# Loading and turning the first batch's keys in two halves of rows, with both sketch matrices on ScalarE's queue

## The chip, the cores and the metric

The kernel runs on one core of a Trainium2 chip. A core has TensorE (PE, matrix products; its weight loads are shown apart as PEld), VectorE (DVE), ScalarE (ACT), GpSimd (POOL) and SyncE (SP, which here only issues DMA transfers). Each engine works through its own instructions in order. ScalarE can issue transfers too. The metric is the device time of the whole program in microseconds, lower is better. A profile is one execution as the hardware profiler saw it; its times are microseconds from the first instruction.

## The reference

An attention with polynomial sketches, and then a SwiGLU block on its output:

```python
def phi(x):                                     # r = 8
    a = np.einsum('rd,bhsd->bhsr', S1, x)
    b = np.einsum('rd,bhsd->bhsr', S2, x)
    return np.einsum('bhsi,bhsj->bhsij', a, b).reshape(*x.shape[:-1], r * r)
q_p, k_p = (phi(q), phi(k))
kv = np.einsum('bhsf,bhsd->bhfd', k_p, v)
z = np.sum(k_p, axis=2)
num = np.einsum('bhsf,bhfd->bhsd', q_p, kv)
den = np.einsum('bhsf,bhf->bhs', q_p, z)[..., None] + 1e-06
attn = num / den
...
g = x @ w_gate                                  # x: attn as (B*S, H*D)
silu = g * (1.0 / (1.0 + np.exp(-g)))
val = x @ w_val
return (silu * val @ w_out)
```

There are 4 batches, 4 heads, 1088 positions and a head dimension of 32; x is 4352 x 128, and the hidden width is 1536. The keys, queries and values are float32. S1, S2 and the three weight matrices come as 64-bit floats; the kernel loads them as raw 64-bit words.

## The kernel before

**Stages.** The attention of batch 0 comes first and as fast as it can, since nothing else can be multiplied before it yields rows of x. Its queries go in three steps of 6, 5 and 6 groups of 64 positions. From the first step on, units of the SwiGLU block (two products, an activation, a product on VectorE) fill TensorE, at first with weights in float32 (L1025), later in split form (L989 to L1002, L1077). The attentions of batches 1 to 3 are woven into that stream. The program is scheduled by hand: the order in which the code calls the engines is their order of work.

**Transfers.** SyncE issues nearly all loads. Its first ones are, in this order: S1 (L201), all keys of batch 0 (`load_k(0)`, L164 and L207), the first third of the queries (L170 and L208), four pieces of the values (L176 and L209), then the first pieces of `wg` and `wv` (L199, called from L1188), the second third of the queries, the second pieces of `wg` and `wv`, and the last third of the queries (L185 to L189). ScalarE issues S2 (L202). The tile `sraw` takes S1 in its rows 0 to 7 and S2 in its rows 8 to 15.

**Layout of the keys.** `kld` has 128 partitions (4 heads by 32) and 36 slots of 32 elements, of which 34 are loaded and the last two are set to zero by GpSimd. The slot number is 9a + c, with a row a of 0 to 3 and a column c of 0 to 8 (NC = 9). The columns are worked on in three thirds, `fpieces`: c0 is columns 0 to 2, c1 is 3 to 5, and `aside` is 6 to 8.

**Sketches.** While the loads run, TensorE is kept busy with small products of a constant (`keep_warm`, L241; 98 of 32 columns and 12 of 64). `narrow` turns the raw words of both sketch matrices into float32: VectorE L263 and L264, ScalarE L268 and L269, VectorE L271, L277, L286. TensorE then copies the result to every head's partitions (L1165), followed by another `keep_warm` block (L1173 to L1175: 2 products of 512 columns, 7 of 32, 6 of 64). VectorE builds `s12`, a block diagonal form, from it (L1177), and ScalarE builds `sq` (L1183, L1184).

**Keys.** `turn_k` (L325) transposes blocks of 32 x 32 of the keys on VectorE, a third of the columns with all four rows at a time, in the order aside, c0, c1. `key_products` (L350) multiplies, for each column, the rows 0 and 1 together and the rows 2 and 3 together (`a` in 0, 2) with `s12`; each such product is two instructions in the profile. `key_copy` brings the result of a third out of PSUM on ScalarE (L368 for aside, L371 for the others). `key_features` forms the outer products: on GpSimd for aside, on VectorE for c0 and c1 (L377). VectorE turns the first queries (L333) between the key turns and these. TensorE multiplies the queries (L445) and then sums the features in the order c0, aside, c1 (L401); ScalarE copies the sums (L1217). `key_values` (L388) multiplies features and values, `totals` (L497) forms numerators and denominators, and `divide` ends with the first rows of x (L539). Between these VectorE also narrows the first weight pieces.

```python
    c0, c1, aside = fpieces
    order = [c for p in (c0, aside, c1) for c in range(*p)]
    for c in (aside, c0, c1):
        turn_k(*c)
    prods = {}
    for t, c in zip(("acc", "g1", "g2"), (aside, c0, c1)):
        ps = bank(t)
        key_products(ps, *c)
        prods[c] = key_copy(ps, *c, aside=(c == aside))
```

Of the kernel before, what the change touches and what calls it, by code (L numbers as in the profile page):

```python
# [19 lines left out]
def kernel(  # L20
# [28 lines left out]
    nc = tc.nc  # L49
    P = nc.NUM_PARTITIONS  # L50
    B, H, S, Dh = q.shape
    R = S1.shape[0]
    D, Dff = moe_w_gate.shape
    NT = B * S
    NX = S // 32
    HX = NX // 2
    NC = (NX + 3) // 4
# [39 lines left out]
    def touch(*which):  # L97
        for i in which:
            clock[0] += 1
            used[i] = clock[0]  # L100
# [11 lines left out]
    def bank(tag=None):  # L112

        if tag is not None:
            i = place[tag]
        else:
            i = place[free_banks[turn[0] % len(free_banks)]]
            turn[0] += 1
        touch(i)
        return PS[:, i, :]  # L120
# [17 lines left out]
    def wide(tag):  # L138
        i = place[tag]
        touch(i, i + 1)  # L140
        return PS[:, i : i + 2, :]
# [7 lines left out]
    sraw = const.tile([2 * R, Dh], S1.dtype, name="sraw")  # L149
# [3 lines left out]
    kld = const.tile([P, 4 * NC, Dh], FP32, tag="kld", name="kld", bufs=1)  # L153
    qld = const.tile([P, 4 * NC, Dh], FP32, tag="qld", name="qld", bufs=1)
    vld = const.tile([P, H, NC, Dh], FP32, tag="vld", name="vld", bufs=1)
    kT = const.tile([P, NC, 4, 32], FP32, tag="kT", name="kT", bufs=1)
# [3 lines left out]
    fpieces = ((0, 3), (3, 6), (6, NC))  # L160
    NRAW = 4

    def load_k(b):
        nc.sync.dma_start(  # L164
            out=kld[:, 0:NX, :], in_=k[b].rearrange("h (pp x) d -> (h pp) x d", pp=32)
        )

    def load_q(b, x0=0, x1=NX):
        src = q[b].rearrange("h (pp x) d -> (h pp) x d", pp=32)
        nc.sync.dma_start(out=qld[:, x0:x1, :], in_=src[:, x0:x1, :])  # L170
# [14 lines left out]
    def load_next():  # L185
# [12 lines left out]
        t = raw[name, i] = stage.tile([P, 3, P], I64, tag="raw", name="raw", bufs=NRAW)  # L198
        nc.sync.dma_start(out=t[:, 0 : c1 - c0, :], in_=part)  # L199

    nc.sync.dma_start(out=sraw[0:R, :], in_=S1)  # L201
    nc.scalar.dma_start(out=sraw[R : 2 * R, :], in_=S2)  # L202

    nc.gpsimd.memset(kld[:, NX : 4 * NC, :], 0.0)
    nc.gpsimd.memset(qld[:, NX : 4 * NC, :], 0.0)
    nc.gpsimd.memset(vld[96:128, :, NC - 2 : NC, :], 0.0)
    load_k(0)  # L207
    load_q(0, 0, 2 * XS)  # L208
    load_v(0, [nc.sync] * 4)  # L209

# [11 lines left out]
        out=ident[:], in_=ident[:], pattern=[[-1, P]], base=0, channel_multiplier=1,  # L222
# [12 lines left out]
    def keep_warm(n, w=TB, ps=None):  # L235


        if ps is None:
            ps = bank(free_banks[turn[0] % len(free_banks)])
        for _ in range(n):  # L240
            nc.tensor.matmul(  # L241
                ps[0:32, 0:w], warm[:, 0:32], warm[:, 0:w], start=True, stop=True
            )
# [78 lines left out]
    s123 = const.tile([P, 2 * H, 3, R], FP32, name="s123")  # L322
    own2 = const.tile([P, 2 * H], FP32, name="own2")
    sq = const.tile([P, 2, R, R], FP32, name="sq")
    def turn_k(c0, c1):  # L325
        four = "p (a c) d -> p a c d"
        nc.vector.transpose(
            out=kT[:, c0:c1, :, :].rearrange("p c a t -> p a c t"),
            in_=kld[:].rearrange(four, a=4)[:, :, c0:c1, :],
        )  # L330

    def turn_q(x0, n):
# [14 lines left out]
                    stop=True,  # L347
                )

    def key_products(ps, c0, c1):  # L350

        for c in range(c0, c1):
            for a in (0, 2):
                nc.tensor.matmul(  # L354
                    ps[32 * a : 32 * a + 64, 64 * (c - c0) : 64 * (c - c0) + 64],
                    kT[:, c, a : a + 2, :].rearrange("p a t -> p (a t)"),
                    s12[:].rearrange("p h t r -> p (h t r)"),
                    start=True,
                    stop=True,
                )  # L360

    def key_copy(ps, c0, c1, aside=False):

        n = c1 - c0
        ab = ps[:, 0 : 64 * n].rearrange("p (x t r) -> p x t r", t=2, r=R)
        if aside:
            kab = apool.tile([P, n * H, 2, R], FP32, tag="kab", name="kab")
            nc.scalar.copy(kab[:], ab)  # L368
            return kab[:, :, 0, :], kab[:, :, 1, :]
        ka = apool.tile([P, n * H, R], FP32, tag="ka%d" % c0, name="ka")  # L370
        nc.scalar.copy(ka[:], ab[:, :, 0, :])  # L371
        return ka[:], ab[:, :, 1, :]
# [194 lines left out]
    def turn_keys(b):  # L567

        for c in kpieces:
            turn_k(*c)  # L570
            if c[1] == NC and b + 1 < B:
                load_k(b + 1)
            yield
# [41 lines left out]
    def attentions():  # L615
# [5 lines left out]
        for i, c in enumerate(kpieces):  # L621
            key_products(kp[:, i, :], *c)
# [24 lines left out]
        kvz = pair("values")  # L647
        key_values(kvz[:, 0, 0:F], phk, 0, NC)
        kab, copies = sketched(pair(), key_products, 2, "kab2")
        run_copies(copies, 2)  # L650
        value_sums(kvz[:, 0, :], zs)
# [18 lines left out]
        for b in (2, 3):  # L670
            yield "pe"
            if b == 3:
                numerators(2, spread)
            kv = bank("g2")
            key_values(kv[:, 0:F], phk, 0, NC)
            if b == 2:
                kab, copies = sketched(pair(), key_products, 2, "kab2")
                run_copies(copies, 2)
            value_sums(kv, zs)
            fold(kv)  # L680
            spread = spread_out(b, kv)
            yield
            yield "pe"
            qab, copies = sketched(pair(), query_sketches, 3, "qab")
            run_copies(copies, 2)
            yield
            if b == 2:
                yield from turn_queries(3)
                phk = late[:, NL - 6 :, :].rearrange("p s (n h i j) -> p (s n) h i j", h=1, i=R, j=R)
                phk = phk.rearrange("p (c h) o i j -> p c (h o) i j", h=H)  # L690
                yield from features(phk, kab)
                zs, sums = feature_sums(phk)
            yield from beside(query_step(b, qab), sums)
# [105 lines left out]
    acc = {}  # L799
# [325 lines left out]
    rows = out.rearrange("(b pp x) (a d) -> b a pp x d", pp=32, x=NX, d=32)  # L1125
# [38 lines left out]
    for h in range(H):  # L1164
# [5 lines left out]
            stop=True,  # L1170
        )
    ps = bank("acc")
    keep_warm(2, ps=ps)  # L1173
    keep_warm(7, 32, ps=ps)
    keep_warm(6, 64, ps=ps)  # L1175
    sTv = srep[:, 0 : 2 * R].rearrange("p (t r) -> p t r", t=2)
# [1 line left out]
        out=s12[:],  # L1178
# [11 lines left out]

    c0, c1, aside = fpieces
    order = [c for p in (c0, aside, c1) for c in range(*p)]
    for c in (aside, c0, c1):
        turn_k(*c)
    prods = {}
    for t, c in zip(("acc", "g1", "g2"), (aside, c0, c1)):
        ps = bank(t)
        key_products(ps, *c)
        prods[c] = key_copy(ps, *c, aside=(c == aside))
    turn_q(*steps[0])  # L1200
    n = steps[0][1]
# [24 lines left out]
    ps = bank("g0")  # L1226
# [8 lines left out]
    ps = bank("g1")  # L1235
# [92 lines left out]
    for z, (i, j) in enumerate(seq):  # L1328
        if z == 17:
            free_banks.pop()  # L1330
            turn[0] %= 4
        unit(i, j)
        for p in parts.get(z, ()):
            part(*p)
        if z == 6:
            load_k(1)
            load_v(1, [nc.sync] * 4)
            load_q(1)
        if z >= 17:
            next_down()  # L1340
            parts_of(1)
        if z == 19:
            catch_up(nc.vector)
            catch_up(nc.vector)
        at(*steps_at.get(z, ()))
# [78 lines left out]
    ps = wide("a")[:, 0, 0:D]  # L1424
# [7 lines left out]
    b, x0 = divmod(t0 // 32, NX)  # L1432
# [34 lines left out]
```

## Time and profile before

| what | value |
| --- | --- |
| median of 3 runs | 276.63 us (276.59 to 276.78) |
| span of the profiled execution | 275.1 us |
| PE busy | 268.8 us, 98% of the span |
| DVE busy | 214.1 us, 78% |
| ACT busy | 193.6 us, 70% |
| POOL busy | 105.7 us, 38% |
| PE in the chain that ended last | 93% |
| mean granted TensorE clock | 0.999 |
| moved by DMA | 14.30 MB, mean 52 GB/s |

The time of a run is taken around the program, the span from its first to its last instruction, so the span is somewhat shorter. The profile's chain is found backwards from the last instruction: at each step to what released it, or to the instruction before it on its engine. A busy share is a mean over the span; what one stage waits for is read from the chain and the timeline of that stage. In a timeline line the first number is the start, the second the time from the first start to the last end of the merged instructions, and in brackets stands how long the engine was idle before, and what ended that.

### The profile page before, as it was taken

What the parts mean: (1) busy time and instruction counts of PE and PEld (TensorE: products, weight loads), DVE (VectorE), ACT (ScalarE), POOL (GpSimd) and SP (SyncE); (2) the same over time, 40 slices, a digit from 0 to 9 for tenths busy, and PEclk for the clock granted to TensorE, in tenths of its full rate; (3) what the DMA queues carried; (4) which work ended last, traced back from release to release, by engine and by line L of the source; (5) the groups of instructions that cost most, each with busy time, mean ns of one, the idle gap of its engine ahead of it and who ended that gap; (6) DMA issues with size and microseconds to landing.
All of it is one profiled execution on the core that took longest, in us unless ns stands there. A gap on an engine that the chain in (4) does not pass through costs nothing.

```text
span 275.1 us, 5788 instructions
## 1 busy us (share of the span) xinstructions
PE 268.8 (98%) x2191; PEld 200.5 (73%) x2191; DVE 214.1 (78%) x373; ACT 193.6 (70%) x349; POOL 105.7 (38%) x117
## 2 busy tenths in 40 slices
PE   7999999999999999999999999999999999999995
PEld 6645566666785786777577777867887888789994
DVE  3997988989788773887545766967987995998871
ACT  2468666462685686677479898769879888897880
POOL 3313422149350640260034353435535663553330
PEclk9999999999999999999999999999999999999999
DMA  6573196122231043000200020000100200010021
GB/s 191 172 216 87 49 270 200 60 104 62 62 88 23 4 111 99 2 0 0 38 12 4 1 38 0 0 2 11 26 2 0 36 1 0 13 25 1 2 36 29
DMA packets 26139, 14.30 MB, mean 52 GB/s; under 512 B 19840, under 2 KB 24192, under 8 KB 26112
## 3 DMA queue, kind: packets, MB, share of 16 engines
q1 hardware_dynamic: 25456, 13.84, 19.6%
q8 instruction: 17, 0.28, 0.4%
q10 hardware_dynamic: 656, 0.10, 0.2%
q14 instruction: 10, 0.08, 0.1%
HBM read 11.41 MB, written 2.23 MB: 50 GB/s over the span
## 4 chain that ended last, share of the span: by engine, by line
PE 93%; DVE 3%; DMA 2%; ACT 1%; issue 0%; SPq 0%
PE PS L1077 20%; PE PS L1001 14%; PE PS L989 14%; PE PS L1002 14%; PE PS L1025 12%; PE PS L1072 3%; PE PS L1071 3%; PE PS L1069 3%; PE PS L354 2%; PE PS L776 2%; PE PS L342 2%; DMA kld<-in_k_dram 2%; PE PS L388 2%; PE PS L1117 1%; PE PS L497 1%; PE PS L445 1%
## 5 line engine op out<-in xcount | busy, mean ns | idle before, releaser
L992 ACT ACTIVATE PS<-PS 128x960 f32<-128x960 f32 (+1 forms) x90 | 83.3, 926 | 29.8 <-PE PS L989 28.8
L1009 DVE SCALAR_TENSOR_TENSOR hbuf<-PS,sg 128x480 f32<-128x480 f32 (+1 forms) x87 | 55.2, 634 | 36.6 <-ACT sg L1004 36.1
L1004 ACT ACTIVATE sg<-PS 128x480 f32<-128x480 f32 (+1 forms) x90 | 49.6, 551 | 1.6 <-PE PS L1002 1.2
L1077 PE MATMUL PS<-hbuf,wo 128*128 128x480 f32 (+2 forms) x94 | 39.4, 516 | 0.0
L989 PE MATMUL PS<-xd,graw 128*128 128x480 f32 (+1 forms) x69 | 37.5, 543 | 0.0
L989 PE MATMUL PS<-xd,wd 128*128 128x480 f32 (+1 forms) x90 | 33.6, 373 | 0.0
L1002 PE MATMUL PS<-x,wb 128*128 128x480 f32 (+1 forms) x90 | 33.5, 372 | 0.0
L1001 PE MATMUL PS<-x,w 128*128 128x480 f32 (+1 forms) x90 | 33.4, 371 | 0.0
L1002 PE MATMUL PS<-x,graw 128*128 128x480 f32 (+1 forms) x69 | 25.5, 370 | 0.0
L989 PEld LDWEIGHTS PS<-xd,wd 128*128 128x128 f32 x90 | 17.0, 189 | 9.9 <-issue 5.3
L1025 PE MATMUL PS<-xT,wg 128*128 128x384 f32 (+1 forms) x60 | 23.5, 473 | 0.1
L1025 PE MATMUL PS<-xT,wv 128*128 128x384 f32 (+1 forms) x60 | 23.2, 467 | 0.3 <-DVE wv L286 0.3
L868 POOL TENSOR_TENSOR x<-xT,x 128x480 fp32r<-128x480 f32 (+1 forms) x6 | 7.2, 1195 | 37.8 <-ACT x L865 37.8
L1077 PEld LDWEIGHTS PS<-hbuf,wo 128*128 128x128 f32 x94 | 17.7, 189 | 5.4 <-issue 0.4
L1029 ACT ACTIVATE sg<-PS 128x384 f32<-128x384 f32 (+1 forms) x24 | 11.2, 468 | 13.2 <-PE PS L1025 12.4
L969 POOL TENSOR_TENSOR hlate<-hbuf,hlate 128x480 fp32r<-128x480 f32 (+1 forms) x12 | 14.6, 1218 | 11.0 <-ACT hlate L968 9.7
L989 PEld LDWEIGHTS PS<-xd,graw 128*128 128x128 f32 x69 | 13.0, 188 | 7.6 <-ACT PS L992 4.1
L1001 PEld LDWEIGHTS PS<-x,w 128*128 128x128 f32 x90 | 16.9, 187 | 2.2
L1002 PEld LDWEIGHTS PS<-x,wb 128*128 128x128 f32 x90 | 16.9, 188 | 2.1
L1001 PE MATMUL PS<-x,graw 128*128 128x480 f32 (+1 forms) x48 | 18.1, 376 | 0.0
L1077 PE MATMUL PS<-hbuf,scaled 128*128 128x480 f32 (+1 forms) x40 | 17.1, 518 | 0.0
L1025 PEld LDWEIGHTS PS<-xT,wv 128*128 128x128 f32 x60 | 11.2, 190 | 7.4 <-DVE hbuf L1040 0.8
(205 smaller groups left out, 572.0 us busy)
## 6 DMA issues: line engine op xcount, KB each, us to landing
kld<-in_k_dram SPq DMA_DIRECT2D x4, 544.0 KB, 4.4
vld<-in_v_dram SPq DMA_DIRECT2D x12, 144.0 KB, 4.3
qld<-in_q_dram SPq DMA_DIRECT2D x3, 544.0 KB, 4.8
raw<-in_moe_w_out_dram SPq DMA_DIRECT2D x4, 384.0 KB, 4.4
raw<-in_moe_w_gate_dram SPq DMA_DIRECT2D x3, 384.0 KB, 3.3
raw<-in_moe_w_val_dram SPq DMA_DIRECT2D x3, 384.0 KB, 3.5
out_dram<-o SPq DMA_DIRECT2D x16, 60.0 KB, 2.0
vld<-in_v_dram SPq DMA_DIRECT2D x4, 112.0 KB, 4.1
```

The lines of the kernel that those rows point to most:

```text
L969: add_to(before, y + 2, lambda: nc.gpsimd.tensor_tensor(out=h0, in0=h, in1=whole(h1), op=ALU.subtract))
L989: nc.tensor.matmul(ps[:, k], w_parts[id(w), j // 3][2][:, j % 3, :], xd, start=True, stop=True)
L992: nc.scalar.activation(ps, ps, AF.Copy, scale=-1.0 / WHOLE)
L1001: nc.tensor.matmul(ps[:, k], w1, x1, start=False, stop=False, skip_group_check=True)
L1002: nc.tensor.matmul(ps[:, k], wb, x0, start=False, stop=True, skip_group_check=True)
L1004: nc.scalar.activation(sg, ps[:, 0], AF.Silu, scale=WHOLE)
L1009: nc.vector.scalar_tensor_tensor(out=hj[:, 0:n], in0=ps[:, 1], scalar=WHOLE, in1=sg, op0=ALU.mult, op1=ALU.mult)
L1025: nc.tensor.matmul(o[:, 0:n], w[:, j, :], xT[:, t0 : t0 + n], start=True, stop=True)
L1029: nc.scalar.activation(sg[:, 0:n], g[:, 0:n], AF.Silu)
L1069: nc.tensor.matmul(acc[i][:, 0:n], wd, hd, **sides)
L1071: nc.tensor.matmul(p, w1, h1, start=(j == mine[0]), stop=False)
L1077: nc.tensor.matmul(acc[i][:, 0:n], w, hidden[i, j][:, 0:n], **sides)
```

## The change

Four things are changed, all in the work on batch 0 before its first features:

- `load_k` takes a range of slots. The keys of batch 0 are loaded by two transfers, slots 0 to 17 (rows a = 0, 1) and slots 18 to 33 (rows a = 2, 3), and these are the first two that SyncE issues. The other batches' keys are loaded whole, as before.
- S1 is issued by ScalarE, after S2.
- The keys are turned by four instructions instead of three: the rows 0 and 1 of all nine columns at once, then the rows 2 and 3 of aside, c0 and c1. TensorE multiplies the rows 0 and 1 of all three thirds first, and then the rows 2 and 3 of each third, after which that third is copied out.
- The second `keep_warm` block has one product of 512 columns instead of two.

```diff
-    def load_k(b):
-        nc.sync.dma_start(
-            out=kld[:, 0:NX, :], in_=k[b].rearrange("h (pp x) d -> (h pp) x d", pp=32)
-        )
+    def load_k(b, x0=0, x1=NX):
+        src = k[b].rearrange("h (pp x) d -> (h pp) x d", pp=32)
+        nc.sync.dma_start(out=kld[:, x0:x1, :], in_=src[:, x0:x1, :])
...
-    nc.sync.dma_start(out=sraw[0:R, :], in_=S1)
+    load_k(0, 0, 2 * NC)
+    load_k(0, 2 * NC, NX)
     nc.scalar.dma_start(out=sraw[R : 2 * R, :], in_=S2)
+    nc.scalar.dma_start(out=sraw[0:R, :], in_=S1)
...
-    load_k(0)
     load_q(0, 0, 2 * XS)
     load_v(0, [nc.sync] * 4)
...
-    def turn_k(c0, c1):
+    def turn_k(c0, c1, rows=slice(0, 4)):
         four = "p (a c) d -> p a c d"
         nc.vector.transpose(
-            out=kT[:, c0:c1, :, :].rearrange("p c a t -> p a c t"),
-            in_=kld[:].rearrange(four, a=4)[:, :, c0:c1, :],
+            out=kT[:, c0:c1, rows, :].rearrange("p c a t -> p a c t"),
+            in_=kld[:].rearrange(four, a=4)[:, rows, c0:c1, :],
         )
...
-    def key_products(ps, c0, c1):
+    def key_products(ps, c0, c1, rows=(0, 2)):
 
         for c in range(c0, c1):
-            for a in (0, 2):
+            for a in rows:
...
     ps = bank("acc")
-    keep_warm(2, ps=ps)
+    keep_warm(1, ps=ps)
     keep_warm(7, 32, ps=ps)
     keep_warm(6, 64, ps=ps)
...
-    for c in (aside, c0, c1):
-        turn_k(*c)
+    sums = dict(zip((aside, c0, c1), [bank(t) for t in ("acc", "g1", "g2")]))
+    turn_k(0, NC, slice(0, 2))
+    for c in sums:
+        turn_k(*c, slice(2, 4))
+    for c, ps in sums.items():
+        key_products(ps, *c, (0,))
     prods = {}
-    for t, c in zip(("acc", "g1", "g2"), (aside, c0, c1)):
-        ps = bank(t)
-        key_products(ps, *c)
+    for c, ps in sums.items():
+        key_products(ps, *c, (2,))
         prods[c] = key_copy(ps, *c, aside=(c == aside))
```

## The prediction

> **What bounds the kernel now.** I read the page first: PE is busy 98% of a 275.1 us span and 93% of the chain that ended last is PE, so a change in the opening is worth what it moves the point from which TensorE no longer waits. Then the chain of waits from 0 to 40 us, in order of time (start, duration, what):
>
> ```profile
> 1.24 4.45 DMA kld<-in_k_dram
> 5.69 0.02 issue
> 5.71 0.59 DVE kT L327
> 6.30 0.04 issue
> 6.34 1.49 PE PS L354 x36
> 7.83 0.92 PE PS L445 x32
> 8.76 0.04 issue
> 8.79 1.49 PE PS L401 x16
> 10.28 0.02 issue
> 10.30 0.38 ACT zq L1217
> ...
> 29.78 10.27 PE PS L1025 x33
> ```
>
> The opening hangs on the keys: 4.45 us from issue to landing, then turn, products, feature sums. From 14.62 to 22.20 this chain is VectorE without a gap, then TensorE to the end. So a shift at 5.71 is carried to the end almost one for one, unless something else arrives last. The timeline of the first 10 us shows what could (start, duration, engine, line):
>
> ```profile
> 0.84 0.57 ACTq L202 DMA_DIRECT2D sraw<-in_S_dram  x1
> ...
> 2.64 0.17 DVE L263 TENSOR_SCALAR exp<-sraw 16x32 int32<-16x32 int32 x1 [2.64 <-DMA sraw<-in_S_dram]
> ...
> 4.20 0.30 PE L1165 MATMUL PS<-ident,s 16*32 16x16 f32 x8
> 4.43 1.20 PE L241 MATMUL PS<-const-bfloat16-1.0 128*32 128x512 bf16 x15
> 4.64 0.23 DVE L1177 TENSOR_TENSOR s<-PS,own 128x64 f32<-128x64 f32 x1 [0.86 <-PE PS L1165]
> ...
> 5.71 1.50 DVE L327 STREAM_TRANSPOSE kT<-kld 128x384 f32<-128x384 f32 x3 [0.85 <-DMA kld<-in_k_dram]
> ```
>
> The sketches' way (landing, L263 to L286, TensorE L1165, VectorE L1177) ends at 4.87 and the keys come 0.85 us later. VectorE works in order and L1177 stands before the turns, in the changed kernel too: no half of the keys can be turned before the sketch matrices have made this whole way. That is the step on which everything turns.
>
> **The keys.** S1's issue (0.82 to 1.18) leaves SyncE's queue, so the keys are issued at 0.82, not 1.24: 0.42 us sooner. Two issues instead of one put the queries' issue back at 1.65, where it was. The first half is 18/34 of 544 KB, 288 KB. From 4 to 6 us the DMA window moves 0.60 MB, 300 GB/s; the other 256 KB cost 0.87 us there. First half: 0.82 + 4.45 - 0.87 = 4.40. Second half: between 0.82 + 4.45 = 5.27 (splitting costs nothing) and 1.24 + 4.45 = 5.69 (its own issue decides); I take 5.40, nearer the first, as the transfers queue behind one another.
>
> **The sketches.** S1 now goes second on ScalarE's queue: S2's issue lasts 0.57, so S1's starts near 0.84 + 0.57 + 0.05 = 1.46 (1.30 if the issue lasts 0.42, as each of ScalarE's two at 271.03 does, 0.88 together). From S2's issue to L263 it is 1.80 us (0.84 to 2.64): 3.26 for the new S1. But the keys are now in the 16 DMA engines before S1's packets; in the trace of before, the sketches' packets went ahead of them. No row shows a small transfer against a bulk one. Bounds: nothing (3.10 with the short issue), or behind the whole first half (4.40 + 0.10 = 4.50). I take one key packet in front, 0.17 us (a steady packet of 4,352 B lasts 0.168 us in the packet records), near the low bound because the two queues are separate: 3.43.
>
> The Trainium skill (DMA: Bandwidth & Descriptors, "Issuing engines are not separate DMA queues") says that DMAs from ScalarE and SyncE end on the same engines and interleave, and its section on queues has an engine finish a whole packet of one queue before it takes another's, some 9 to 17 descriptors. This speaks against the change: by it S1 would stand behind about a first half per engine, and the sum would go to the 4.50 above.
>
> From L263 on: 2.64 to 3.78 is 1.14; 0.06 to TensorE (as from a turn's end 6.29 to its product 6.34); L1165 to L1177 0.44 (4.20 to 4.64); 0.20 to the next VectorE instruction (L1177 lasts 0.23 and overlaps a little). 3.43 + 1.14 + 0.06 + 0.44 + 0.20 = 5.27 is T, the start of the first turn, against 5.71. Both key halves are covered: the first lands 0.87 before T, and the second's turns start at T + 0.70 = 5.97, 0.57 after its landing. With that cover gone the second half's delay would count in full. Were the halves not told apart and the first turn waited for all keys, T would be 5.42.
>
> **Turns and products.** Before, three turns of 384 elements start 0.47 apart ((7.13 - 5.71)/3); six products of a third start 0.058 apart after a first gap of 0.10; first product 0.16 after the turn's slot. TensorE is fed by the turns there, not the limit. After: a turn of 576 takes 0.70, three of 192 take 0.24 by proportion, or 0.30 if each has a fixed part; the four end 0 to 0.2 later than three, covered by what follows. Products of the first rows start at T + 0.70 + 0.16 = T + 0.86; nine of them end their starts at T + 1.37, and only then come those of the second rows: aside to T + 1.54, c0 to T + 1.72. The copy of a finished third starts 0.27 after its last product (6.69 to 6.96): aside T + 1.81, where before it was 1.25 after the first turn. GpSimd's features start 0.47 later (6.96 to 7.43) and last 1.51: T + 3.79. ScalarE's next copy comes at T + 2.03 and lasts 0.24; VectorE's two features start at T + 2.30 (before: 7.69, 1.98 after the turn) and last 1.82: T + 4.12. So the third of the sums that waited 0.19 for VectorE at 9.56 comes at T + 4.17, against 3.85 after the turn before: a lag of 0.32. By GpSimd's way (3.79 + 0.05 + 0.45 for the aside sums) it is T + 4.29, 0.44. I take 0.38. Splitting by rows thus costs what it was to save: every third is finished only after all the first rows.
>
> **What else moves.** One 512-column warm-up is gone (0.40 of TensorE, off the path: TensorE idles 0.71 before 6.34). SyncE's own waits (waited for, total, times, longest):
>
> ```profile
> SPq L199 <- DMA kld<-in_k_dram: 1.2, 1, 1.2
> SPq L199 <- DMA vld<-in_v_dram: 0.4, 1, 0.4
> ```
>
> The first weight of wv, at 5.70, waits for the keys' landing, eight transfers back counting the keys' own issue and ScalarE's; wv's second, at 7.41, for the first v. With one transfer more, the last v will stand behind the first key half (3.56 to about 4.4) and the first wg behind the second (4.03 to about 5.4), with every later load queued behind them on SyncE. I cost it at nothing: the v pieces need 5.3 to 5.6 us to land, so the engines have work waiting, and the last v lands at 9.16 against a first use at 9.80; wv's second lands at 11.5, is used at 11.70, and VectorE idles 0.27 after it, so 0.46 of cover. If that were gone, the delay beyond 0.46 would count; the same cover caps a gain at about half a microsecond.
>
> **Sum:** 5.27 + 0.38 - 5.71 = -0.06 us. The profiled execution spans 275.1, the median is 276.63, 1.5 us around it; the shift is the same in both: 276.57, say 276.6. The bounds of S1's landing give -0.39 (T = 4.94) and +1.01 (T = 6.34). The likeliest case's own range is 276.2 to 277.1. A difference of 0.2%, 0.55 us, is about what a measurement here can tell.
>
> **Rivals.**
> - S1 caught behind the keys. It decides from T = 5.88 on, L263 at 4.04. For it: keys now start first, and both halves, q and v fill the engines. Against: separate queues, 4 KB in all. At the bound +1.01: 277.6. Chance 0.25.
> - The gain kept whole. S1 undisturbed (T = 4.94), and no lag, if the copies and products overlap better than by these rows: -0.77, 275.9. Against: in-order TensorE and ScalarE. Chance 0.12.
> - A slower TensorE. S1 later leaves TensorE idle from 4.26 to about 4.63, and the warm-up behind is shorter. The granted clock reads 1.00 in every window from 0.80 to 10.30, so no row prices it; from nothing to both groups doubled (1.49 + 0.92 = 2.4). Products are fed at half TensorE's pace, which hides part: I take +0.6, 277.2. Chance 0.13.
> The skill (TensorE: Matmul & The Clock Gate, Part 1) gives full clock after about 3.4 us of sustained work in a free-running window. By that rule a pause before the grant could put it off a window; no row here shows one.
>
> **How the numbers follow.** Forecast 0.50 (of it 0.46 within 0.2%, 0.01 faster, 0.03 slower); S1 caught 0.25, slower; gain kept 0.12 (0.10 faster, 0.02 same); slow clock 0.13 (0.07 slower, 0.06 same). Faster 0.11, same 0.54, slower 0.35. The range, 276.0 to 277.7, leaves out the bottom of the kept gain and the far tail of the two slower cases.
>
> **What would show it.** L263 at 3.4 (4.0 or later: the first rival); the first L327 at 5.3, 0 to 0.1 after L1177 and not ended by a DMA; a turn of 0.7 and three of 0.25; first copy 1.8 after the first turn; L401's last third 4.2 after it; SyncE's fourth v waiting for a key half; 512-column warm-ups and L354 at their old durations. Wrong if VectorE waits for keys, if L263 starts before 3.1, or if a weight piece ends a VectorE wait between 10 and 13 us.

## The result, and the profile after

The changed kernel takes 279.0 us (median of 7 runs, 277.75 to 279.3) against 276.75 for the kernel before in the same session (7 runs, 276.59 to 276.83). The ratio is 1.0064, with a 95% interval of 1.0044 to 1.0084 (an estimate over the runs, not the quotient of the two medians, which is 1.0081): slower by less than 1%, clear of the noise, and outside the range of the forecast. Its runs lie on two levels, three at 277.75 to 278.16 and four at 279.00 to 279.30; the profiled execution, of 277.4 us span, is one of the upper level.

The chain of waits of the changed kernel, in order of time (start, duration, what):

```profile
1.47 2.55 DMA sraw<-in_S_dram
...
5.40 0.28 PE PS L1165 x5
...
5.77 0.22 DVE s L1177
6.00 0.70 DVE kT L327
6.70 0.04 issue
6.74 3.56 PE PS L354 x36
10.30 0.89 PE PS L445 x32
11.19 1.44 PE PS L401 x16
12.63 0.02 issue
12.65 0.38 ACT zq L1220
```

The keys have left the chain. It now begins with S1, issued at 1.47 and landed at 4.02, goes through the whole way of the sketches, and then spends 3.56 us in the key products that took 1.49. The copy of the feature sums (L1217 before, L1220 now) starts at 12.65 instead of 10.30: 2.35 us later, and the span is 2.3 us longer. Nothing behind that point adds or gives back: everything happened in the first 13 us.

The timeline of the same stretch (start, duration, engine, line; in brackets the idle time before and what ended it):

```profile
4.12 0.17 DVE L263 TENSOR_SCALAR exp<-sraw 16x32 int32<-16x32 int32 x1 [4.12 <-DMA sraw<-in_S_dram]
...
5.40 0.25 PE L1165 MATMUL PS<-ident,s 16*32 16x16 f32 x8 [1.37 <-DVE s L286]
...
5.92 1.55 DVE L327 STREAM_TRANSPOSE kT<-kld 128x576 f32<-128x576 f32 x4
...
9.06 0.32 ACT L368 COPY kab<-PS 128x192 f32<-128x192 f32 x1 [2.70 <-PE PS L354]
...
9.97 1.82 DVE L377 TENSOR_TENSOR phk<-ka,PS 128x768 f32<-128x768 f32 x2 [2.04 <-ACT ka L371]
```

The first turn starts at 5.92, released by VectorE's own L1177 and not by a transfer; before it was 5.71. TensorE stood still for 1.37 us before L1165. ScalarE's first key copy comes 3.14 us after the first turn (9.06 - 5.92), where it came 1.25 after it before (6.96 - 5.71).

The clock over that time (window, its length, busy time of PE, PEld, DVE, ACT and POOL with the number of instructions, then granted clock, DMA share, GB/s):

```profile
5.40:6.98 1.58, 1.17 (x26) 0.90 (x27) 1.21 (x4) 0.33 (x2) 0.00 (x0) 1.00 1.06 234
6.98:10.39 3.41, 3.41 (x44) 3.29 (x50) 1.36 (x4) 0.61 (x3) 0.86 (x1) 0.50 0.98 307
10.39:12.50 2.11, 2.11 (x61) 1.49 (x65) 2.11 (x4) 1.05 (x3) 1.25 (x5) 1.00 0.03 11
```

For 3.41 us, from 6.98 to 10.39, the granted clock was 0.50, and this stretch covers nearly all key products. So there are three candidates for the loss: the late S1, the order of the products, and the clock.

### The profile page after: what moved, and what is told of

Read it like the earlier page. It is cut to its first block, busy times and chain, and to the rows that moved or that the text cites. A ratio compares the mean times of both kernels' runs of the same rounds, so it can differ in the third digit from the quotient of the medians.

```text
span 277.4 us, 5788 instructions
## 1 busy us (share of the span) xinstructions
PE 270.1 (97%) x2190; PEld 202.2 (73%) x2190; DVE 214.0 (77%) x374; ACT 193.5 (70%) x349; POOL 105.5 (38%) x117
## 4 chain that ended last, share of the span: by engine, by line
PE 93%; DVE 4%; DMA 1%; ACT 1%; issue 0%; DVEq 0%
PE PS L1077 20%; PE PS L1001 14%; PE PS L989 14%; PE PS L1002 14%; PE PS L1025 12%; PE PS L1069 3%; PE PS L1071 3%; PE PS L1072 3%; PE PS L354 3%; PE PS L776 2%; PE PS L342 2%; PE PS L388 2%; PE PS L1117 1%; DMA sraw<-in_S_dram 1%; PE PS L497 1%; PE PS L445 1%
```

## The experiments

Nine further kernels, and a second profile of two kernels, tell them apart; the time that each is compared with is that of the kernel before on the same chip.

**1. S1 back in front.** The changed kernel, with S1 issued by SyncE first; the rest of the change stays.

```diff
+    nc.sync.dma_start(out=sraw[0:R, :], in_=S1)
     load_k(0, 0, 2 * NC)
     load_k(0, 2 * NC, NX)
     nc.scalar.dma_start(out=sraw[R : 2 * R, :], in_=S2)
-    nc.scalar.dma_start(out=sraw[0:R, :], in_=S1)
```

> The changed kernel with S1 issued by SyncE ahead of the two key halves again; key halves, split turns and the shorter warm-up stay. Theory 1 (the changed kernel loses because S1 on ScalarE's queue arrives behind the keys, at 4.02 instead of about 2.5, which delays the first turn to 5.92 and leaves TensorE idle from 4.02 to 5.40, after which its clock is halved from 6.98 to 10.39): L263 at 2.6 to 2.7, L1165 at 4.2, first turn at 4.9, no half clock, and 4.9 + 0.38 - 5.71 = -0.4 us against before, 276.3. Rival (the order by rows, with every third finished late, is the main loss): no better than 277.5, with ScalarE's first key copy more than 2.2 us after the first turn.

276.86 us (11 runs, 276.74 to 277.5) against 276.69, ratio 1.0006 (0.9995 to 1.0017). The pause and the half clock over the key products are gone, and so is nearly all of the loss; but the gain of 0.4 us is not there. The timeline of this kernel:

```profile
4.64 0.23 DVE L1177 TENSOR_TENSOR s<-PS,own 128x64 f32<-128x64 f32 x1 [1.05 <-PE PS L1165]
4.78 1.54 DVE L327 STREAM_TRANSPOSE kT<-kld 128x576 f32<-128x576 f32 x4
...
5.60 2.13 PE L354 MATMUL PS<-s,kT 128*64 128x64 f32 x36 [0.18 <-DVE kT L327]
...
7.07 0.32 ACT L368 COPY kab<-PS 128x192 f32<-128x192 f32 x1 [1.85 <-PE PS L354]
```

The first turn starts at 4.78, 0.93 us sooner than before, in time for both halves of the keys. But the 36 passes take 2.13 us for 1.49, with TensorE never waiting, the first copy starts 2.29 after the first turn, above the 2.2 that was the rival's mark, and the copy of the sums starts at 10.30, exactly where it was. The rival's time was wrong and its mark right: turning and multiplying by rows eats what the early keys bring, 0.93 us.

**2. The pause filled.** The changed kernel with more warm-up ahead of the sketches.

```diff
-    keep_warm(12, 64)
+    keep_warm(48, 64)
...
-    keep_warm(1, ps=ps)
+    keep_warm(2, ps=ps)
```

> The changed kernel with 48 instead of 12 warm-up products of 64 columns ahead of the sketches, and two products of 512 columns after them as before, so that TensorE is busy in most of the pause from 4.02 to 5.40. Theory (two losses: the late start of the first turn, and on top of it the half clock that follows from the pause): no half clock behind 6 us, key products at 0.058 us each, and about before + 0.2 (first turn 5.92 for 5.71) + 0.4 (lag of the order by rows) = 277.3. Rival (the half clock has nothing to do with the pause, or costs little): the clock is 0.50 again for 3.4 us, or the time stays above 278.3 with a full clock.

278.25 us (5 runs, 278.19 to 278.4) against 276.69, ratio 1.006 (1.0048 to 1.0072): one level, with L354 at the 2.13 us of the first experiment, and the clock record of the trace at 1.00 from its first entry, at 4.88, on. The clock is part of the loss, then, and follows the pause. The remaining loss is larger than the 0.6 us expected: the first turn starts at 6.15, as the filling delays L1165 to 5.62, and the copy of the sums comes 5.53 after it (11.68), as in the first experiment (5.52) and not 4.59 as before. 0.44 and 0.94 make 1.38 of the 1.56; the rest stays unexplained.

**3. Only S1 moved.** The kernel before, with the keys as one transfer first on SyncE's queue.

```diff
-    nc.sync.dma_start(out=sraw[0:R, :], in_=S1)
+    load_k(0)
     nc.scalar.dma_start(out=sraw[R : 2 * R, :], in_=S2)
+    nc.scalar.dma_start(out=sraw[0:R, :], in_=S1)
...
-    load_k(0)
     load_q(0, 0, 2 * XS)
```

> The kernel before, but the whole keys are SyncE's first transfer and S1 goes behind S2 on ScalarE's queue; one key transfer, turns and products by thirds, warm-up as before. Theory (S1 loses its place ahead of the keys): L263 at 3.9 to 4.5, TensorE idle for more than 1 us before L1165, first turn after 5.7 and released by L1177 and not by the keys, 277.3 if the clock stays full and 278.5 to 279.5 if it falls to half. Rival (the keys' packets delay S1 only because they are split into smaller ones, and whole keys do not): L263 below 3.4 and a time within 0.4 us of before, or less than it, as the keys come 0.4 us sooner.

278.95 us (6 runs, 277.47 to 280.62) against 276.69, ratio 1.0087 (1.006 to 1.0114). The move alone makes the kernel as slow as the whole change. S1 is later still behind undivided keys:

```profile
4.89 0.17 DVE L263 TENSOR_SCALAR exp<-sraw 16x32 int32<-16x32 int32 x1 [4.89 <-DMA sraw<-in_S_dram]
...
6.18 0.30 PE L1165 MATMUL PS<-ident,s 16*32 16x16 f32 x8 [1.91 <-DVE s L286]
...
6.75 1.49 DVE L327 STREAM_TRANSPOSE kT<-kld 128x384 f32<-128x384 f32 x3
```

2 KB issued at 1.47 landed at 4.80 behind 544 KB issued at 0.82; the rival, that whole keys do not delay it, is out. The loss is not the late S1 alone. Here too the key products ran at half pace (shortest, median and longest pass in ns, first and last start; the median before is 222):

```profile
L354 PE MATMUL PS<-s,kT x36: 271/314/369, 7.9 to 9.8; 128*64 128x64 f32 x36
```

The copy of the sums starts at 12.36, 2.06 us later than before: 1.04 for the first turn, and 1.02 from there on, with turns and products ordered as before.

**4. Only the order by rows.** The kernel before, with the products of rows 0 and 1 of all thirds ahead of those of rows 2 and 3.

```diff
...
     prods = {}
-    for t, c in zip(("acc", "g1", "g2"), (aside, c0, c1)):
-        ps = bank(t)
-        key_products(ps, *c)
+    sums = dict(zip((aside, c0, c1), [bank(t) for t in ("acc", "g1", "g2")]))
+    for c, ps in sums.items():
+        key_products(ps, *c, (0,))
+    for c, ps in sums.items():
+        key_products(ps, *c, (2,))
         prods[c] = key_copy(ps, *c, aside=(c == aside))
```

> The kernel before with one part of the change alone: TensorE multiplies the rows 0 and 1 of all three thirds first and then the rows 2 and 3; loads, turns by thirds and warm-up as before. Theory (products that alternate between rows 0 and 2 go to two halves of TensorE's columns and run two at a time, a pair of passes every 0.058 us; products of the same rows in a row take 0.058 us for each pass): 36 passes with no two starts 0.007 us apart except where the rows change, first product 6.34, last start about 8.66 for 7.61, ScalarE's first key copy at 8.2 for 6.96, VectorE's first features at 8.8 for 7.69, and 1.1 to 1.2 us more than before, 277.8. Rival (the pairs of before are two passes of one product, and the order by rows only finishes the thirds later): last start about 7.7, first copy at 7.4, no more than 0.4 us slower.

277.55 us (6 runs, 277.36 to 277.58) against 276.63, ratio 1.003 (1.0019 to 1.0042): 0.92 us by itself, where 1.1 to 1.2 were expected.

```profile
5.50 1.50 DVE L327 STREAM_TRANSPOSE kT<-kld 128x384 f32<-128x384 f32 x3 [0.63 <-DMA kld<-in_k_dram]
...
6.13 2.35 PE L354 MATMUL PS<-s,kT 128*64 128x64 f32 x36 [0.30 <-DVE kT L327]
...
7.82 0.32 ACT L368 COPY kab<-PS 128x192 f32<-128x192 f32 x1 [2.59 <-PE PS L354]
```

The first copy comes 2.32 us after the first turn for 1.25, as expected (8.2 less 5.71 is 2.49; the keys came 0.2 us sooner here). The single starts say why. Before, they go in pairs: 0.007 us from the first of a pair to the second, 0.052 to the next pair. Here there are no pairs except where the rows change: 0.058 us from each start to the next while TensorE does not wait for a turn. So what I had taken for two passes of one product must be one pass each of two products, of rows 0 and of rows 2, in TensorE at the same time: two passes of one product would still come in pairs here.

**5. Only the pause.** The kernel before with less warm-up at the start.

```diff
-    keep_warm(98, 32)
+    keep_warm(50, 32)
```

> The kernel before with 50 instead of 98 warm-up products of 32 columns, so that TensorE pauses for about 1.5 us before the sketches and nothing else changes. Theory (a pause of more than a microsecond in the opening costs the full clock for a stretch of 3.4 us): the profile has the clock at 0.50 somewhere between 4 and 11 us, where key products take 0.107 us a pair of passes, and the time is 0.5 to 1.5 us above before in most runs. Rival (the clock of the changed kernel fell because of the late products, not the pause): full clock by 5 or 6 us and a time within 0.2 us of before.

278.73 us (6 runs, 277.31 to 278.89) against 276.63, ratio 1.0063 (1.0047 to 1.0079); the profiled run took 278.07. No work is added and no transfer late; TensorE's pause before L1165 was 0.74 us, not the 1.5 expected. The lines that show it, from the key products in this kernel and in the one before (engine, operation, count: shortest, median, longest in ns, first and last start):

```profile
L354 PE MATMUL PS<-s,kT x36: 314/314/369, 6.3 to 8.2; 128*64 128x64 f32 x36
```

```profile
L354 PE MATMUL PS<-s,kT x36: 222/222/270, 6.3 to 7.6; 128*64 128x64 f32 x36
```

Each pass lasts 314 ns for 222, and the pairs start 0.107 us apart for 0.058. The first profile of the changed kernel has the same 314 as its median, inside the stretch for which the clock reads 0.50. The copy of the sums starts at 11.54 after a first turn at 5.66: 1.29 us more than before. The expected 0.50 does not appear in this profile: its granted clock reads 1.00 in every window, although the key products plainly run at half pace. The reason is in the trace: its clock record has no entry before 10.09, and the windows read 1.00 where there is none. A 1.00 ahead of the first entry is thus no proof of a full clock; the duration of a known pass is.

The same holds for the kernel before. Its first entry is at 4.95, and its warm-up products of 64 columns start 0.053 us apart until 4.03 and 0.031 apart from 5.32 on: it too began at half pace, but had the full clock before its key products. The first entry lies between 3.84 and 6.06 in the nine profiles of the kernel before and of the experiments without such a pause. In this one it is at 10.09, with only S1 moved at 9.86, and in the second profile of the changed kernel, below, at 9.04.

**6. The changed kernel again**, for a second profile.

> The changed kernel once more, for a second profile. Theory (the runs near 278.0 are those whose clock stays full, the runs near 279.1 those with a stretch at half): a time below 278.4 goes with a full clock over the key products and 36 passes in 2.1 us; a time above 278.8 with a clock of 0.50 there and 36 passes in 3 us or more. Rival: the two levels have the same clock.

278.99 us, and much the same: 36 passes in 3.11 us, the copy of the sums 6.50 us after the first turn (12.48 - 5.98; 6.73 in the first profile). The passes that start up to 9.0 run at half pace:

```profile
L354 PE MATMUL PS<-s,kT x24: 271/314/368, 6.8 to 8.9; 128*64 128x64 f32 x24
```

The other 12 last 222 ns and start 0.058 us apart, from 9.05 on; the first entry of the clock record, at 1.00, is at 9.04. So in this run the full clock came late, whereas in the first profile it had come at 3.56 and was taken back from 6.98 to 10.39.

```profile
6.80 2.77 PE PS L354 x30
9.57 0.02 issue
9.60 0.25 ACT ka L371
9.85 0.02 issue
9.87 0.97 DVE phk L377
```

In the chain of this run too the key products stand between the turn and ScalarE. A run of the lower level was not profiled, so that its key products run at the full clock is argued from the sum below, not shown.

**7. What the late S1 costs alone.** The changed kernel with its pause filled as in the second experiment, and its products by thirds again.

```diff
-    for c, ps in sums.items():
-        key_products(ps, *c, (0,))
     prods = {}
     for c, ps in sums.items():
-        key_products(ps, *c, (2,))
+        key_products(ps, *c)
```

> The changed kernel with its pause filled (48 warm-up products of 64 columns, two of 512 behind the sketches) and its products by thirds again, rows 0 and 2 in turn; keys first in two halves, both sketches on ScalarE's queue. What is left of the change is the late S1. Theory (the order by rows costs 0.95 us at a full clock, the late S1 the rest of what the filled kernel lost): first turn at 6.0 to 6.2, key products 1.3 to 1.5 us, ScalarE's first copy 1.8 to 1.9 after the first turn, about 0.95 us less than the filled kernel's 278.25, 277.2 to 277.4. Rival (the products are bound by something else, so that their order doesn't matter behind a late start): 278 or more.

277.99 us (12 runs, 277.25 to 278.44) against 276.56, ratio 1.0043 (1.0029 to 1.0057). The median lies between theory and rival. The profiled run took 277.25:

```profile
5.72 1.55 DVE L327 STREAM_TRANSPOSE kT<-kld 128x576 f32<-128x576 f32 x4
...
6.54 1.52 PE L354 MATMUL PS<-s,kT 128*64 128x64 f32 x36 [0.20 <-DVE kT L327]
...
7.40 0.32 ACT L368 COPY kab<-PS 128x192 f32<-128x192 f32 x1 [1.24 <-PE PS L354]
```

Here the products take 1.52 us and the copy of the sums comes 4.91 us after the first turn (10.63 - 5.72): 0.32 more than before, the price of turning by rows in four instructions, and 0.62 less than with the order by rows (5.53). The clock record reads 1.00 from 3.84 on. Why most of its runs are slower than the profiled one was not looked into; the first turn depends on S1's landing and on the filling, which gave 5.72 here and 6.15 in the second experiment.

**8. Keys in two transfers, and nothing else**, as a version that might beat both.

```diff
-    load_k(0)
+    load_k(0, 0, 2 * NC)
+    load_k(0, 2 * NC, NX)
     load_q(0, 0, 2 * XS)
```

> The kernel before, with S1 first as there, but the keys in two transfers of 18 and 16 slots; turns and products by thirds, warm-up as before. Theory (two transfers land sooner than one: in the changed kernel the second half landed at 4.3, 3.4 us after the first issue, where the whole keys took 4.45): second half landed by 4.9, first turn at 4.9 to 5.0, released by L1177, and 0.7 to 0.8 us less than before, 275.9 to 276.1. Rival (the sooner landing came from the place ahead of S1 and from chance): first turn at 5.5 to 5.8 and within 0.2 us of before.

276.55 us (12 runs, 275.92 to 277.25) against 276.69, ratio 0.999 (0.9975 to 1.0005): unclear. The first turn does start at 4.78, as the theory has it, but the 0.8 us are not there:

```profile
4.78 1.49 DVE L327 STREAM_TRANSPOSE kT<-kld 128x384 f32<-128x384 f32 x3
...
7.61 0.58 DVE L333 STREAM_TRANSPOSE qT<-qld 128x384 f32<-128x384 f32 x1 [1.35 <-DMA qld<-in_q_dram]
```

The queries, issued at 2.13 for 1.65, landed at 7.6 in this run of 277.25, and VectorE waits 1.35 us for them. The copy of the sums starts at 10.74, 0.44 later than before. A second profile of the same kernel:

> The kernel with S1 first and the keys in two transfers, once more, for a second profile, as its times spread from 275.92 to 277.25. Theory (the spread is the queries' landing, which came at 7.6 in the profile of 277.25): a time below 276.4 goes with VectorE's query turn before 7.0, one above 277 with a turn after 7.4. Rival (the spread is the clock): the time goes with how long the clock stays at half after 5 us, whatever the queries do.

276.24 us beside 276.48, and there the query turn starts at 6.26 without a wait, the copy of the sums at 9.75, 0.55 sooner than before. The theory holds for these two profiles, taken on two chips: the slower one waited for the queries, and the clock, the rival, had its first entry at 6.06 and 5.94, nearly the same. The other eleven runs were not looked into.

The faster one shows what else holds the gain back:

```profile
4.43 1.54 PE L241 MATMUL PS<-const-bfloat16-1.0 128*32 128x512 bf16 x15
...
4.84 1.50 DVE L327 STREAM_TRANSPOSE kT<-kld 128x384 f32<-128x384 f32 x3
...
5.90 1.27 PE L354 MATMUL PS<-s,kT 128*64 128x64 f32 x36
```

The first turn is 0.87 us sooner than before, but TensorE is busy with the warm-up block behind the sketches until the key products start, 1.06 after the first turn, where it was 0.63. Early keys with a shorter block, and the products by thirds, were not run.

**9. Two ways to bring the queries forward**: the second half of the keys, or the first queries, on ScalarE's queue behind S2. Both have S1 first and the keys in two transfers.

```diff
+    load_k(0, 2 * NC, NX, nc.scalar)        # the first version
...
+    load_q(0, 0, 2 * XS, nc.scalar)         # the second version
```

> A version meant to beat both: the kernel before with S1 first on SyncE's queue and the keys in two transfers, the first half second on SyncE's queue and the other half on ScalarE's, behind S2, so that the queries' issue stays at 1.65; turns and products by thirds. Theory (the keys' landing and then the queries' are what waits): first turn at 4.8, queries landed by 6.7, VectorE's first features at 7.1 to 7.2 for 7.69, 0.4 to 0.6 us less than before. Rival (the queries' landing is set by the volume ahead of them and not by their issue): queries landed after 7.2 and within 0.2 us of before.

> A version meant to beat both: S1 first on SyncE's queue, then the keys in two transfers on the same queue; the first third of the queries on ScalarE's queue behind S2; turns and products by thirds, warm-up as before. Theory (with the keys in time for a first turn at 4.8, the queries' landing is what waited in the kernel with only two transfers, at 7.6): queries landed by 6.2, first turn at 4.8 to 5.2, VectorE's first features at 6.8 to 7.3 for 7.69, 0.4 to 0.8 us less than before. Rival (the two queues share the same engines, so that the keys lose what the queries gain, as in the kernel with the second half on ScalarE's queue): first turn after 5.5 and within 0.2 us of before.

276.79 us (11 runs) against 276.63, ratio 1.0009 (0.9999 to 1.0019), and 277.94 us (12 runs) against 276.56, ratio 1.0043 (1.0026 to 1.0061). The first turns of the two:

```profile
5.70 1.50 DVE L327 STREAM_TRANSPOSE kT<-kld 128x384 f32<-128x384 f32 x3 [0.87 <-DMA kld<-in_k_dram]
```

```profile
6.45 1.50 DVE L327 STREAM_TRANSPOSE kT<-kld 128x384 f32<-128x384 f32 x3 [1.59 <-DMA kld<-in_k_dram]
```

Both theories fell. What goes beside the keys on the other queue delays them: the first half took 3.5 us from issue to landing in both, where it took 2.7 and 2.9 in the two profiles of the eighth experiment, and the first turn falls back to 5.70 and to 6.45. The second version is slower than even its rival had it. No version clearly beats the kernel before.

## Why the prediction was wrong

The opening can now be added up at one mark, the copy of the feature sums: 10.30 before, 12.65 after. Later first turn: 5.92 - 5.71 = 0.21. Turning and multiplying by rows, at a full clock: 5.52 (first experiment) - 4.59 = 0.93, of which 0.32 for the four turns and 0.61 for the order (seventh). Half clock: 6.73 - 5.52 = 1.21 (0.98 in the second profile). Together 2.35, which has to come out, as the last term is what the others leave. What tests the terms is outside the sum: by itself the order costs 0.92, and the half clock of the fifth experiment 1.44 in its profiled run; with S1 back in front 0.17 is left. The split of the 0.93 goes by the sequence in which the two parts are taken: with the turns of before, the order alone costs 0.96 at this mark (fourth). Without the half clock the sum is 1.14 above 276.75, 277.9, where the lower level of runs lies (277.75 to 278.16).

Point by point:

- That the opening carries to the end almost one for one: right, 2.35 us at 12.65 and 2.3 in the span.
- **The keys' landing**: the direction right, the size too small. The halves landed 2.8 and 3.0 us after issues at 0.82 and 1.27, so at 3.6 and 4.3, where 4.40 and 5.40 were put. It earned nothing, as VectorE's order stood before it, which was said: the first turn was released by L1177.
- **S1 behind the keys**: "I take one key packet in front, 0.17 us" failed. L263 started at 4.12, not 3.43: beyond the 3.26 without keys it was 0.86. The packet records show what stood in front: the 128 packets of the first half start from 1.83 to 3.20, S1's eight packets of 256 bytes from 3.22 to 3.53. S1 went behind the whole first half, not behind one packet. The way from there to the first turn was put at 1.84 and took 1.80. The page of the Trainium skill that was weighed (DMA: Bandwidth & Descriptors) spoke for just such a wait, behind about a first half per engine, and the packets agree with it; the 4.50 that the sum would have gone to was too late because the first half landed at 3.6 and not at 4.40. The third experiment, 4.89 behind undivided keys, shows the same dependence. The first rival's mark, L263 at 4.04, was passed.
- **The lag of the order by rows**: "six products of a third start 0.058 apart" is the step that failed worst, since it is a misreading. 12 passes of a third start in six pairs, and I counted a pair as one product. Nine products of the first rows are 18 passes of 0.058 with no partner, twice what I allowed; the first copy comes 2.29 after the first turn at a full clock, not 1.81, and the lag is 0.93, not 0.38. The Trainium skill (TensorE: Matmul & The Clock Gate, Part 3) says that products which use different column tiles of the array run at the same time, with starts some 4 ns apart. The starts in pairs agree with it, 7 ns apart before and 4 to 5 in the faster profile of the eighth experiment, and the fourth experiment shows what losing them costs: 0.92 us.
- **The clock**: held a rival with chance 0.13 and priced at 0.6; it cost 1.21. It was argued away with the granted clock at 1.00 "in every window from 0.80 to 10.30", of which the windows ahead of 4.95 had no entry behind them; the warm-up's starts, 0.053 us apart there and 0.031 later, would have told. The price was too small because "Products are fed at half TensorE's pace, which hides part" does not hold: the six pairs of a third take 0.35 us of the 0.46 between two turns at the full clock, and 0.64 at the half clock. The fifth experiment, with products in pairs, lost 1.29 by it: 0.70 of this by the end of the key products (8.48 - 5.66 against 7.83 - 5.71), the rest in the query products and sums behind them. And the two rivals were added as if they excluded each other, though the late S1 is what makes the pause.
- **SyncE's waits** at nothing: right. The fourth v did not wait for a key half. The first wg load stood behind the second half, as forecast, but moved only from 4.03 to 4.33, with 0.2 us of waiting, and nothing waited for it.

The range ended at 277.7 because each slower case was priced alone. In the profiled runs a late S1, a larger lag and a half clock came together.

## What to carry to other kernels

Before putting a large load in front of a small one, ask whose way is longer: the sketches had a way through VectorE, ScalarE and TensorE to go after landing and the keys none, so the small transfer had to lead, and another queue did not protect it. When products are reordered, look at single starts in the trace: in this case pairs a few nanoseconds apart were two products at work at once, and an order that broke the pairs needed 0.058 us for each pass instead of for each pair. A pause of about a microsecond in the opening (0.74 to 1.91 us here) can cost more than the wait that caused it.

## What had not been expected of the hardware

- Two transfers of 18 and 16 slots land sooner than one of 34: first turn at 4.78 and 4.84 with S1 ahead of both, 5.50 to 5.71 with one transfer (5.71, 5.50, 5.66 in three profiles). With the keys ahead of everything, the second half landed at 4.3 and the undivided keys, in the third experiment, at 4.8.
- In the first profile of the changed kernel the clock record reads 1.00 from 3.56, 0.50 from 6.98 and 1.00 from 10.39 on, in steps of 3.41 us; the pause of 1.37 us lies inside the first step. The Trainium skill (TensorE: Matmul & The Clock Gate, Part 1) names windows of about 3.4 us, and the steps agree.
- One pass of 128x64 lasts 222 ns at the full and 314 at the half clock, and starts 0.058 and 0.107 us after the one before it.
- The same landing differs from run to run by more than the changes looked at here: the first queries let VectorE go on by 6.26 and at 7.61 in two runs of one kernel, on two chips.
